# One turn of k^T v instead of two, and the gate's columns copied together with it

## The chip, the cores and the metric

The kernel runs on one core of one Trainium2 chip. The metric is the device time of one execution in microseconds (us). Times given as the kernel's time are medians over several executions; a profile shows one execution alone.

## What is computed

Linear attention without a softmax for 8 batches and 8 heads (576 positions, 64 columns a head), an RMS norm per head, and then a mixture of 8 experts on the 512 joined columns:

```python
kv = np.einsum('bhsd,bhse->bhde', k, v)
out = np.einsum('bhsd,bhde->bhse', q, kv)
rms = np.sqrt(np.mean(out * out, axis=-1, keepdims=True) + 1e-06)
x = out / rms * g_norm                   # heads joined to 512 columns
logits = np.einsum('bsd,de->bse', x, w_gate)
local_gate = 1.0 / (1.0 + np.exp(-np.einsum('bsd,de->bse', x, w_local).squeeze(-1)))
# per position: the best expert if local_gate < 0.5 or s == 0, else the expert of the position before
h = np.maximum(x[b, s] @ w1[e], 0.0)
out[b, s] = p[e] * (h @ w2[e])           # p: softmax of the logits
```

## The kernel before

There are two stages. The first computes attention, the gate and the routing, and writes rows to a table `xs` in DRAM. The second gathers rows by expert and multiplies them with the experts' matrices.

The first stage runs in 16 steps `s` (NST). A step takes two batches and two heads, that is 4 products of 64x64 each. `kv(s)` multiplies k^T v into PSUM (tile `po`) and copies it to `kvp`: on partitions 64y to 64y+63, in column block x, stands the product of head x and batch x xor y. Each of the two heads' products is needed on both halves of the partitions, since q, turned by `turn_q` and `turn_last` into `qT` and `ql`, has even and odd positions on different halves. `kvb_of(s, t)` therefore copies `kvp` to half t of `kvb`, in two copies of 64 partitions on POOL (GpSimd), one per y.

Beside the 64 columns of each product `kvb` has NG = 9 more: the product times the gate's columns (8 experts and the local gate). So the multiplication q (k^T v) in `q_kv` delivers the logits, before the norm's factor, with the output. They are made from k^T v turned by 90 degrees: `turn_kv` turns `kvp` (128x128) on PE and ACT copies the result to `kq`; before the change it turns it twice, for each half t of the output partitions anew, so that `kq` has the product twice, side by side. `logits_of` multiplies `kq` with `gw`, the gate's columns scaled by `g_norm`, once for each half, into `pm`; two copies on ACT put the 2 x 9 columns each beside the products in `kvb`, on all 128 partitions.

PE, ACT (ScalarE), DVE (VectorE) and POOL follow an order written out by hand: the string `STEP` has one letter for each piece of work of step i, `LATE` has other strings for the last three steps, and `work_of` says what a letter does:

- Q, a: the first part of q (k^T v) for step i, and its copy to `raw`; c, R: the second part, and its copies
- K, k: k^T v for step i+2 on PE, and its copy to `kvp`; K also issues the loads of k and v for step i+4
- V: turns `kvp` of step i+2 and copies it to `kq`
- L, l: the logits product of step i+1 on PE, and its copy on ACT
- 0, 1: `kvb_of` for step i+1, halves 0 and 1
- T, U: turn q of step i+1; e: load q for step i+3
- x, y, X, Y: squares of the output for the norm, on POOL or on ACT; s: their sums on DVE
- p, m, q, b: pieces of norm, gate and routing of a finished group of four steps; w, v: split a piece of an expert's matrix; o: store three rows' blocks and load a piece
- G, 2, 3, 4, 5: the first two gathers for the experts, and their scaling and turning

Loads and stores are issued on SP in the order of the program; at most 7 are under way at a time (`LANES`). PSUM has three buffers for the tiles `pq`, `pl`, `pt`, `pm` (`ps_q`) and two for `po`. `HW` is 64 + 9 = 73, `XO` is 9, `slot(x, b)` is the column in `kvb` at which head x of batch b begins, and `pair` views two equal pieces of a tile at a fixed distance.

Of the kernel before, what the change touches and what calls it, by code (L numbers as in the profile page):

```python
# [8 lines left out]
F32 = mybir.dt.float32  # L9
# [13 lines left out]
def kernel(  # L23
# [12 lines left out]
    nc = tc.nc  # L36
    P = 128
    B, H, S, D = q.shape
# [3 lines left out]
    NG = E + 1  # L42
# [5 lines left out]
    NP = H // 2  # L48
    HW = D + NG
    PW = 2 * HW  # L50
    KB = PW - NG
    XO = NG
    NGRP = B // 2
    NCH = NGRP * C
    NST = NGRP * NP
# [23 lines left out]
    ident = const.tile([P, P], F32, name="ident")  # L79
# [63 lines left out]
    KVB, LGC = "PP", "A"  # L143
# [5 lines left out]
    wk = work.enter_context(tc.tile_pool(name="wk", bufs=2, reuse_waits="tile"))  # L149
# [10 lines left out]
    for src, e0 in ((w_gate, 0), (w_local, E)):  # L160
# [8 lines left out]
    ps_q = ps1.enter_context(tc.tile_pool(name="ps_q", bufs=3, space=PSUM,  # L169
                                           reuse_waits="tile"))  # L170
# [134 lines left out]
    gw = rc.tile([P, NP, 2 * NG], F32, name="gw")  # L305
# [55 lines left out]
    kvps, kvbs, kqs, qTs, qls = {}, {}, {}, {}, {}  # L361

    def half(b):
        return slice(b * D, (b + 1) * D)

    def kv(s):


        pk = ps_o.tile([P, 2, 512], F32, name="po")
        ks, vs = ([t.pop((s, b)) for b in range(2)] for t in (kts, vts))  # L370
        for c in range(C):
            cd = slice(c * D, (c + 1) * D)
            for b in range(2):
                for x in range(2):
                    nc.tensor.matmul(pk[half(x ^ b), x, 0:D], ks[b][half(x), cd],  # L375
                                     vs[b][half(x), cd], start=(c == 0), stop=(c == C - 1))
        yield
        kvps[s] = wk.tile([P, 2, D], F32, name="kvp")
        nc.scalar.copy(kvps[s], pk[:, :, 0:D])  # L379
        yield  # L380

    def pair(t, o0, o1, n):

        w = o1 - o0
        return t[:, o0:o0 + 2 * w].rearrange("p (x w) -> p x w", w=w)[:, :, 0:n]


    def slot(x, b):
        return (2 * (x ^ b) + x) * HW

    def kvb_of(s, t):

        if s not in kvbs:
            kvbs[s] = wk.tile([P, 2 * HW + 2 * (HW + D)], F32, name="kvb", bufs=3)
        for y in range(2):
            copy[KVB[t]](pair(kvbs[s][half(t)], slot(0, y) + XO, slot(1, 1 - y), D),  # L396
                         kvps[s][half(y)])

    copy = {"A": nc.scalar.copy, "D": nc.vector.tensor_copy, "P": nc.gpsimd.tensor_copy}

    def turn_kv(s):

        pt = ps_q.tile([P, 2, P], F32, name="pt", tag="pq")
        kvp = kvps[s].rearrange("p x d -> p (x d)")
        for t in range(2):
            nc.tensor.transpose(pt[:, 0:2, half(t)], kvp, ident)
        kqs[s] = wk.tile([P, 2, P], F32, name="kq", bufs=3)
        nc.scalar.copy(kqs[s], pt)

    def turn_last(s):  # L410
# [6 lines left out]

    def logits_of(s):

        pm = ps_q.tile([P, 2, 2 * NG], F32, name="pm", tag="pq")  # L420
        for y in range(2):
            nc.tensor.matmul(pm[:, y], kqs[s][:, y], gw[:, s % NP], start=True, stop=True)
        yield
        for y in range(2):
            copy[LGC](pair(kvbs[s], slot(0, y), slot(1, 1 - y) + D, NG),
                      pm[:, y].rearrange("p (x e) -> p x e", x=2))
        yield

    def turn_q(s, b):
# [410 lines left out]
    LOADED = {i: j for j, i in enumerate((1, 2, 3, 4, 5, 9, 13, 14))}  # L840
    SPLIT = {i: j for j, i in enumerate((4, 5, 7, 8, 10, 12, 15))}

    STEP = "QKasw1p0kcRTUeqLlmvVxobY"
    LATE = {NST - 3: "QKswLpck01qaRmGXVvlYbTUeo", NST - 2: "QKLmapkRUcT10q2lVe3Ysxbo", NST - 1: "5Q4wRcvsaxyO"}

    SLOTS = {}
    for g in range(NGRP - 1):
# [11 lines left out]
    def work_of(i, what):  # L859
# [16 lines left out]
        elif what in "ac" and now:  # L876
            next(step[what])
            done.add((i, what))
        elif what == "K" and new:
            step["k"] = kv(i + 2)  # L880
            next(step["k"])
            for b in range(2):
                load_kv(i + 2 + LB, b)
        elif what == "k" and new:
            next(step["k"])
        elif what == "L" and nxt:
            step["l"] = logits_of(i + 1)
            next(step["l"])
        elif what == "l" and nxt:
            next(step["l"])  # L890
        elif what in "01" and nxt:
            kvb_of(i + 1, int(what))
        elif what == "T" and nxt:
            for b in range(2):
# [3 lines left out]
        elif what == "e" and nxt:  # L898
            assert i + 1 in qls and i + 1 in qTs
            for b in range(2):  # L900
                load_q(i + 1 + LQ, b)
        elif what == "V" and new:
            turn_kv(i + 2)
        elif what == "w" and i in SPLIT:
            step["v"] = wsplit(0, SPLIT[i], True)
# [30 lines left out]
    for i in range(-2, NST):  # L936
        if i == NST - 1:
            paced.clear()
        if i == NST - 2:
            xb = rw.tile([P, C, NP * PW], F32R, name="raw", bufs=3).rearrange("p c w -> p (c w)")  # L940
            xh, xl = (xb[:, o:o + ND * 2 * P].rearrange("p (d t) -> p d t", d=ND)
                      for o in (0, ND * 2 * P))
        for what in LATE.get(i, STEP):
            work_of(i, what)
# [518 lines left out]
```

## Time and profile before

| what | value |
|---|---|
| median of 3 runs | 583.35 us (582.9 to 585.02) |
| the profiled execution's own time | 580.4 us |
| its span on the core | 578.6 us |
| PE busy | 540.2 us (93%) |
| PE weight loads busy | 480.8 us (83%) |
| DVE, ACT, POOL busy | 306.9, 239.2, 235.3 us |
| DMA packets | 41380, 94.97 MB, mean 164 GB/s |

The span is the stretch of the profiled execution that the profiler shows; the execution's own time is 1.8 us longer. In rows of the profile, L12 is line 12 of the kernel; PE is the matrix engine's products, PEld its weight loads; `out<-in` names the tiles; `[x <-y]` is the idle time of the engine just before, and what ended it; "issue" is waiting for nothing that the profile shows. A product of 32-bit numbers stands as two weight loads and two matmuls, a transposition as one of each.

### The profile page before, as it was taken

How to read it: one execution, taken by the hardware profiler on the slowest of the kernel's cores; microseconds unless marked ns; L12 is line 12 of the kernel's file. 1: busy time of each engine (PE TensorE's matmuls, PEld its weight loads, DVE VectorE, ACT ScalarE, POOL GpSimd, SP SyncE). 2: the span in 40 equal slices, each digit the busy share in tenths (PEclk: the TensorE clock that was granted, in tenths of full speed). 3: DMA queues.
4: the chain of work that ended last, by engine and by line, in shares of the span. 5: the costliest groups of instructions: out<-in, count | busy, mean ns of one | idle time of the engine just before them, and what ended most of it. 6: DMA issues, size and time to landing. Idle time of an engine off the chain costs nothing. (4 is left out here: it accounts for less than half of the span.)

```text
span 578.6 us, 12798 instructions
## 1 busy us (share of the span) xinstructions
PE 540.2 (93%) x5157; PEld 480.8 (83%) x5157; DVE 306.9 (53%) x627; ACT 239.2 (41%) x435; POOL 235.3 (41%) x303
## 2 busy tenths in 40 slices
PE   2987978779999999999999999999999999999996
PEld 2876866759887989899898998989898979999895
DVE  1126578688866633725363755374546545564510
ACT  1567767472244433332343343333433333435220
POOL 4233454133236725434363573456344734442001
PEclk9988899799999999999999999999999999999999
DMA  7999999871657344233443343345343533432000
GB/s 227 342 316 355 295 375 376 291 248 52 237 194 284 102 159 143 89 104 105 130 124 112 110 154 97 123 137 162 86 132 115 172 98 123 145 105 80 18 20 30
DMA packets 41380, 94.97 MB, mean 164 GB/s; under 512 B 7263, under 2 KB 7263, under 8 KB 41312
## 3 DMA queue, kind: packets, MB, share of 16 engines
q1 hardware_dynamic: 32032, 72.64, 36.7%
q0 software_dynamic: 7744, 21.41, 12.4%
q8 instruction: 42, 0.69, 0.5%
q10 hardware_dynamic: 1536, 0.02, 0.1%
q14 instruction: 26, 0.21, 0.1%
HBM read 73.85 MB, written 20.86 MB: 164 GB/s over the span
## 5 line engine op out<-in xcount | busy, mean ns | idle before, releaser
L780 POOL DMA_INDIRECT xr<-xs,gid x120 | 132.1, 1101 | 36.6 <-issue 33.6
L1032 DVE SCALAR_TENSOR_TENSOR hl<-ph,hh 128x384 fp32r<-128x384 f32 (+3 forms) x92 | 52.2, 568 | 115.4 <-ACT hh L1031 111.9
L997 POOL DMA_INDIRECT out_dram<-ot,sidr x34 | 33.8, 994 | 176.9 <-ACT ot L996 136.3
L1031 ACT ACTIVATE hh<-ph 128x384 fp32r<-128x384 f32 (+3 forms) x92 | 47.0, 510 | 124.4 <-PE ph L967 124.4
L996 ACT ACTIVATE ot<-py,pe 128x512 f32<-128x512 f32 (+1 forms) x37 | 25.5, 689 | 70.5 <-PE py L967 31.9
L495 POOL TENSOR_TENSOR sq<-raw 128x576 f32<-128x576 f32 x16 | 19.3, 1210 | 59.4 <-ACT raw L465 30.8
L375 PE MATMUL po<-vt,kt 64*64 64x64 f32 x1152 | 26.6, 243 | 14.1 <-DMA vt<-in_v_dram 10.8
L500 DVE TENSOR_REDUCE ms<-sq 128x9 f32<-128x576 f32 x32 | 23.1, 748 | 28.1 <-POOL sq L495 22.1
L375 PEld LDWEIGHTS po<-vt,kt 64*64 64x64 f32 x1152 | 24.4, 157 | 14.8 <-issue 10.3
L456 PE MATMUL po<-kvb,qT 64*64 64x73 f32 x1024 | 29.2, 246 | 7.5 <-issue 6.7
L456 PEld LDWEIGHTS po<-kvb,qT 64*64 64x64 f32 x1024 | 23.6, 148 | 13.6 <-issue 9.0
L396 POOL COPY kvb<-kvp 64x128 f32<-64x128 f32 x64 | 22.4, 349 | 16.3 <-ACT kvp L379 10.2
L462 ACT COPY raw<-po 128x876 f32<-128x876 f32 (+1 forms) x32 | 20.7, 648 | 19.7 <-PE po L456 19.1
L808 DVE TENSOR_TENSOR xr<-xr 128x512 f32<-128x512 f32 x37 | 25.4, 686 | 0.2 <-DMA xr<-xs,gidr 0.2
L801 ACT CAST yh<-xT 128x512 fp32r<-128x512 f32 x17 | 10.5, 620 | 29.5 <-DVE xT L797 29.5
L961 PE MATMUL py<-w_0h,hh 128*128 128x512 f32 (+1 forms) x56 | 22.2, 397 | 0.0
L966 PE MATMUL py<-w_0l,hh 128*128 128x512 f32 (+1 forms) x56 | 22.1, 394 | 0.0
L961 PE MATMUL py<-w_1h,hh 128*128 128x512 f32 (+1 forms) x56 | 22.1, 394 | 0.0
L967 PE MATMUL py<-w_0h,hl 128*128 128x512 f32 (+1 forms) x56 | 22.0, 393 | 0.1
L435 PE MATMUL pq<-ident,qt 128*128 128x128 f32 x128 | 19.5, 295 | 2.6 <-DMA wst<-in_moe_w_dram 2.1
L966 PE MATMUL py<-w_1l,hh 128*128 128x512 f32 (+1 forms) x56 | 21.9, 391 | 0.0
L967 PE MATMUL py<-w_1h,hl 128*128 128x512 f32 (+1 forms) x56 | 21.8, 390 | 0.0
(433 smaller groups left out, 1661.0 us busy)
## 6 DMA issues: line engine op xcount, KB each, us to landing
wst<-in_moe_w_dram SPq DMA_DIRECT2D x64, 512.0 KB, 3.7
xs<-raw SPq DMA_DIRECT2D x36, 292.0 KB, 5.4
kt<-in_k_dram SPq DMA_DIRECT2D x32, 288.0 KB, 5.2
vt<-in_v_dram SPq DMA_DIRECT2D x32, 288.0 KB, 5.2
qt<-in_q_dram SPq DMA_DIRECT2D x32, 288.0 KB, 5.1
xr<-xs,gid POOLq DMA_INDIRECT x120, 4.5
out_dram<-ot,sidr POOLq DMA_INDIRECT x36, 4.0
xr<-xs,gidr POOLq DMA_INDIRECT x6, 5.5
```

Of the source, the lines that this page charges most:

```text
L375: nc.tensor.matmul(pk[half(x ^ b), x, 0:D], ks[b][half(x), cd], vs[b][half(x), cd], start=(c == 0), stop=(c == C - 1))
L456: nc.tensor.matmul(po[half(b), r, o:o + HW], lhsT[half(r), half(x)], kvb[half(r), slot(x, b):slot(x, b) + HW], start=True, stop=True)
L500: nc.vector.tensor_reduce(mss[g][:, :, 2 * n + x], sqs.pop((s, x)), axis=AX.X, op=ALU.add)
L780: i = nc.gpsimd.indirect_dma_start(out=xr[:, u * PW:(u + 1) * PW], out_offset=None, in_=xs.rearrange("t (q w) -> (t q) w", w=PW), in_offse ...
L808: (engine or nc.vector).tensor_mul(xv, xv, r.unsqueeze(3).to_broadcast([P, NP, 2, D]))
L961: mm = nc.tensor.matmul(ps, ah, bh, start=(first and i == 0), stop=False)
L966: nc.tensor.matmul(ps, ah, bl, start=False, stop=False)
L967: nc.tensor.matmul(ps, al, bh, start=False, stop=(last and i == n - 1))
L996: nc.scalar.activation(ot[0:m], po[0:m], AF.Copy, scale=pe[0:m])
L997: return nc.gpsimd.indirect_dma_start(out=outf, out_offset=bass.IndirectOffsetOnAxis(ap=idx[0:m], axis=0), in_=ot[0:m], in_offset=None, bo ...
L1031: nc.scalar.activation(hh, ps, AF.Relu)
L1032: nc.vector.scalar_tensor_tensor(hl, ps[:, :, 0:nl], 0.0, hh[:, :, 0:nl].bitcast(F32), op0=ALU.max, op1=ALU.subtract)
```

## The change

`turn_kv` turns k^T v once, and `kq` has 128 columns instead of 256. `logits_of` multiplies it once, into 2 x 9 columns, and one copy on ACT puts these beside the products in `kvp`, which has room for them now: 9 columns ahead of the first product and 9 behind the second. `kvb_of` then copies products and logits together, 146 neighbouring columns instead of twice 64, and so follows the logits' copy now. In `STEP` the logits product (L) moves from behind the turning of q to behind k^T v (K), its copy (l) moves from the end of the step to behind the copy of k^T v (k), and the copies to the halves (1, 0) come behind that. `LATE` is changed likewise.

```diff
-        kvps[s] = wk.tile([P, 2, D], F32, name="kvp")
-        nc.scalar.copy(kvps[s], pk[:, :, 0:D])
+        kvps[s] = wk.tile([P, 2 * (HW + D)], F32, name="kvp")
+        nc.scalar.copy(kvps[s][:, XO:XO + 2 * D].rearrange("p (x d) -> p x d", x=2), pk[:, :, 0:D])
...
     def kvb_of(s, t):
+        assert s in lgs
         if s not in kvbs:
-            kvbs[s] = wk.tile([P, 2 * HW + 2 * (HW + D)], F32, name="kvb", bufs=3)
+            kvbs[s] = wk.tile([P, 4 * HW], F32, name="kvb", bufs=3)
         for y in range(2):
-            copy[KVB[t]](pair(kvbs[s][half(t)], slot(0, y) + XO, slot(1, 1 - y), D),
-                         kvps[s][half(y)])
+            copy[KVB[t]](kvbs[s][half(t), slot(0, y):slot(0, y) + 2 * HW],
+                         kvps[s][half(y), 0:2 * HW])
...
     def turn_kv(s):
-        pt = ps_q.tile([P, 2, P], F32, name="pt", tag="pq")
-        kvp = kvps[s].rearrange("p x d -> p (x d)")
-        for t in range(2):
-            nc.tensor.transpose(pt[:, 0:2, half(t)], kvp, ident)
-        kqs[s] = wk.tile([P, 2, P], F32, name="kq", bufs=3)
+        pt = ps_q.tile([P, P], F32, name="pt", tag="pq")
+        nc.tensor.transpose(pt, kvps[s][:, XO:XO + 2 * D], ident)
+        kqs[s] = wk.tile([P, P], F32, name="kq", bufs=3)
         nc.scalar.copy(kqs[s], pt)
...
     def logits_of(s):
-        pm = ps_q.tile([P, 2, 2 * NG], F32, name="pm", tag="pq")
-        for y in range(2):
-            nc.tensor.matmul(pm[:, y], kqs[s][:, y], gw[:, s % NP], start=True, stop=True)
+        pm = ps_q.tile([P, 2, NG], F32, name="pm", tag="pq")
+        nc.tensor.matmul(pm.rearrange("p x e -> p (x e)"), kqs[s], gw[:, s % NP],
+                         start=True, stop=True)
         yield
-        for y in range(2):
-            copy[LGC](pair(kvbs[s], slot(0, y), slot(1, 1 - y) + D, NG),
-                      pm[:, y].rearrange("p (x e) -> p x e", x=2))
+        copy[LGC](pair(kvps[s], 0, HW + D, NG), pm)
+        lgs.add(s)
         yield
...
-    STEP = "QKasw1p0kcRTUeqLlmvVxobY"
-    LATE = {NST - 3: "QKswLpck01qaRmGXVvlYbTUeo", NST - 2: "QKLmapkRUcT10q2lVe3Ysxbo", NST - 1: "5Q4wRcvsaxyO"}
+    STEP = "QKLaswpkl01cRTUeqmvVxobY"
+    LATE = {NST - 3: "QKLswpckl01qaRmGXVvYbTUeo", NST - 2: "QKLmapkl01RUcTq2Ve3Ysxbo", NST - 1: "5Q4wRcvsaxyO"}
```

More of the change, by code (lines that the diff above doesn't have):

```diff
@@ L391, in kvb_of @@
     def kvb_of(s, t):
+        assert s in lgs
         if s not in kvbs:
-            kvbs[s] = wk.tile([P, 2 * HW + 2 * (HW + D)], F32, name="kvb", bufs=3)
+            kvbs[s] = wk.tile([P, 4 * HW], F32, name="kvb", bufs=3)
         for y in range(2):
-            copy[KVB[t]](pair(kvbs[s][half(t)], slot(0, y) + XO, slot(1, 1 - y), D),
-                         kvps[s][half(y)])
+            copy[KVB[t]](kvbs[s][half(t), slot(0, y):slot(0, y) + 2 * HW],
+                         kvps[s][half(y), 0:2 * HW])
+    lgs = set()
     copy = {"A": nc.scalar.copy, "D": nc.vector.tensor_copy, "P": nc.gpsimd.tensor_copy}
     def turn_kv(s):
-        pt = ps_q.tile([P, 2, P], F32, name="pt", tag="pq")
-        kvp = kvps[s].rearrange("p x d -> p (x d)")
-        for t in range(2):
-            nc.tensor.transpose(pt[:, 0:2, half(t)], kvp, ident)
-        kqs[s] = wk.tile([P, 2, P], F32, name="kq", bufs=3)
+        pt = ps_q.tile([P, P], F32, name="pt", tag="pq")
+        nc.tensor.transpose(pt, kvps[s][:, XO:XO + 2 * D], ident)
+        kqs[s] = wk.tile([P, P], F32, name="kq", bufs=3)
         nc.scalar.copy(kqs[s], pt)
```

## The prediction

> **What bounds the kernel now.** I read the page's first line, then the busy time by stretches, to see in which stretch a saved microsecond counts.
>
> ```profile
> span 578.6 us, 12798 instructions
> ```
> ```profile
> 17.00:107.00 90.00, 72.67 (x2119) 63.65 (x2114) 48.52 (x103) 61.60 (x153) 33.21 (x64) 0.94 0.98 345
> 107.00:129.00 22.00, 18.34 (x362) 15.56 (x361) 16.81 (x44) 14.69 (x39) 7.58 (x14) 0.85 0.72 232
> 129.00:578.60 449.60, 443.46 (x2540) 396.66 (x2540) 239.48 (x473) 161.00 (x241) 188.43 (x173) 1.00 0.38 121
> ```
>
> The columns are length, busy PE, weight loads, DVE, ACT, POOL (count in brackets), granted clock, DMA share, GB/s. From 129 us on, the experts' products keep PE busy 443.46 of 449.60 us at full clock: the change touches nothing there, so whatever the attention stage ahead of it wins or loses reaches the end whole. In that stage PE is busy 72.67 of 90 us while DMA is at 0.98. Which of them sets the pace? PE's own list of waits over the first 130 us says what PE lacked (columns: total us, times, longest).
>
> ```profile
> PE po L375 <- DMA vt<-in_v_dram: 10.8, 4, 5.6
> PE po L456 <- issue: 9.8, 5, 3.1
> ```
> ```profile
> PEld po L456 <- ACT kvb L425: 3.6, 14, 0.3
> PEld pm L422 <- ACT qT L436: 3.0, 11, 0.4
> ```
>
> ```profile
> 15.08 2.19 PE L375 MATMUL po<-vt,kt 64*64 64x64 f32 x68 [1.67 <-DMA vt<-in_v_dram]
> ```
>
> The waits for v are four, and this is the last: after some 15 us the loads are ahead of PE. The two small ones with ACT are the ones the change touches: 3.6 us for logits copied into `kvb`, 3.0 us for a free PSUM buffer of the logits. The large one is "issue", in which PE waits for nothing that the profile names. I cut the stretch where those gaps end, and asked for the DMA queues of the first 130 us.
>
> ```profile
> q8 instruction: 20, 0.33, 1.0%
> ```
> ```profile
> 58.77:73.60 14.83, 14.00 (x382) 12.39 (x381) 8.67 (x23) 11.96 (x31) 6.41 (x13) 0.88 0.91 304
> ...
> 84.44:89.26 4.83, 4.60 (x127) 4.02 (x127) 2.17 (x5) 3.84 (x10) 2.30 (x5) 1.00 1.05 382
> 89.26:94.90 5.64, 4.64 (x127) 4.06 (x127) 4.91 (x16) 5.30 (x14) 2.38 (x5) 1.00 1.04 364
> 94.90:101.10 6.20, 4.61 (x128) 3.90 (x128) 5.55 (x12) 3.40 (x10) 2.40 (x5) 1.00 1.05 392
> 101.10:106.94 5.84, 2.79 (x127) 2.57 (x127) 3.25 (x9) 2.00 (x3) 0.00 (x0) 0.98 1.05 386
> sum 80.94, PE 64.16 PEld 56.41 DVE 47.57 ACT 55.06 POOL 29.75; mean PE 5.83 PEld 5.13 DVE 4.32 ACT 5.01 POOL 2.70
> ```
>
> Between two such gaps PE always runs 127 or 128 weight loads and as many matmuls (three times that in the first row): 256 instructions. Queue q8 brought 20 packets of together 0.33 MB, so 16 KB each, one for every 256. PE stops at these boundaries until the next piece of its program has come through DMA engines that are full. From 26 to 107 us there are 15 pieces in 80.94 us, 5.40 us each, while PE is busy only 64.16 us. So over most of that stretch the pace is the arrival of PE's instructions, some 5 to 6 us a piece, and what PE saves inside a piece becomes a longer stop, unless pieces hold more work. The three pieces from 58.77 on, 4.94 us each, were hardly delayed: there PE's own work is the pace.
>
> [...]
>
> **The change part by part.** For each of 16 pair-steps:
>
> ```profile
> 23.51 0.38 PE L414 MATMUL pl<-ident,qt 128*128 128x128 f32 x2
> 23.91 0.62 PE L422 MATMUL pm<-gw,kq 128*128 128x18 f32 x4
> 24.40 0.44 PE L406 MATMUL pt<-ident,kvp 128*128 128x128 f32 x2
> 24.85 0.68 PE L456 MATMUL po<-kvb,qT 64*64 64x73 f32 x25
> ```
>
> (1) PE loses one transposition of two (L406) and two of the four records of L422 (one logits product of two). That is 3 pairs of weight load and matmul a step. From 23.91 to 24.85 logits, transposition and the two waits take 0.94 us. Without them the next Q.KV could follow the transpositions of q by about 0.35 us (two of L414's rank and one of L406's; L422's remaining half moves ahead to a place where PE would else run on, about 0.25). So PE alone could gain up to 0.94 - 0.35 = 0.6 us a step.
>
> (2) Is something else late then? The same place in a later step, ACT and POOL beside it:
>
> ```profile
> 63.90 0.27 ACT L379 COPY kvp<-po 128x128 f32<-128x128 f32 x1 [0.21 <-PE po L375]
> ...
> 65.10 1.07 ACT L436 COPY qT<-pq 128x512 f32<-128x512 f32 x2
> ...
> 66.45 1.58 POOL L396 COPY kvb<-kvp 64x128 f32<-64x128 f32 x4
> 66.49 0.26 ACT L425 COPY kvb<-pm 128x18 f32<-128x18 f32 x2
> ...
> 66.82 0.99 PE L456 MATMUL po<-kvb,qT 64*64 64x73 f32 x48
> ```
>
> The second qT copy ends at 66.17, and Q.KV needs it: it can start at about 66.2 instead of 66.82, and if the logits copy, now ahead of qT's copies on ACT, pushes them by its 0.18, at 66.35. So 0.5 to 0.6 us a step is all that there is; the next thing late is ACT's qT. I take 0.5.
>
> (3) The added wait: POOL's copies to the halves (0, 1) now wait for ACT's logits copy, which stands behind kvp's copy. ACT is done with both at 63.90 + 0.27 + 0.18 = 64.35. POOL's four copies, at some 0.33 us with their gaps, are through by 65.75 (the wider 146 columns at worst 146/128 of that, 65.9): before qT at 66.17, so at nothing. Behind them on POOL stand the square product of the step (up to 1 us later than now, for sums that DVE reads a step afterwards), and in the late steps the gathers (next part). Behind the logits copy on ACT stand the copies of Q.KV's second part and of qT: the 0.18 above. POOL's added columns come to at most 64 x 0.05 = 3 us in all, beside other work. ACT's shorter turned copy (256 to 128 columns) and one small copy less are a gain that I count in (2). The logits product early on PE needs the turned copy of the step before, long done after Q.KV and K.V. No DMA is added, removed or passed on SP; `kvb` shrinks and `kvp` grows, with no load in it.
>
> (4) How much survives the stops? Start of the chain: the first delayed boundary follows one or two steps of PE-paced work: +0.5 us (0 to 1.0). The pieces not delayed, four or so: each holds 0.8 of a step, so up to 0.4 us apiece, 1.6 in all; I take 0.4, as shortening them meets the arrival time soon. Then the pieces hold more work. By the last delayed boundary, in step 12, the changed kernel has dropped 14 transpositions and 26 products' pairs: 40 pairs. At the mean pace that is 40/128 x 5.40 = 1.7 us. But what these 40 pairs are at that boundary can be read off:
>
> ```profile
> 106.95 0.75 PE L456 MATMUL po<-kvb,ql 64*64 64x73 f32 x8 [3.05 <-issue]
> 107.63 1.97 PE L435 MATMUL pq<-ident,qt 128*128 128x128 f32 x8
> 109.39 0.63 PE L414 MATMUL pl<-ident,qt 128*128 128x128 f32 x2
> ...
> 111.13 0.65 PE L456 MATMUL po<-kvb,qT 64*64 64x73 f32 x12
> ```
>
> After the stop of 3.05 us they take from 106.95 to 111.13, 4.2 us, at half speed (L414's two take 0.63 against 0.38 above). With the boundary moved 40 pairs on, this work, its ACT copies included, falls into what is now the 3.05 us stop and the next Q.KV begins near the boundary. So this term lies between 1.7 and 4.2; I take 3.6, near the row that shows the very work, less 0.6 for instructions that come later because q loads and stores move into the full DMA stretch (pieces above vary by 4.83 to 6.20).
>
> (5) The tail. The transposition L414 at 109.39 releases the last q loads on SP, behind which stand row stores and a weight load, and the gathers on POOL wait for the stores:
>
> ```profile
> 117.66 1.23 POOL L770 DMA_INDIRECT xa<-xs,gi  x1 [6.76 <-DMA wst<-in_moe_w_dram]
> ...
> 123.66 0.74 POOL L396 COPY kvb<-kvp 64x128 f32<-64x128 f32 x1 [3.11 <-DMA xa<-xs,gi]
> ```
>
> So what step 12 wins moves the gather, and with it the last copies to `kvb`, which wait for the landed gather before and after the change. The logits copy no longer follows them: about 0.25 us.
>
> **Sum:** 0.5 + 0.4 + 3.6 + 0.25 = 4.75 us, bounds 0 + 0 + 1.7 + 0 and 1.0 + 1.6 + 4.2 + 0.4. The profiled execution took 580.4, its span and 1.8 around it, so 575.65; the median of the runs is 2.95 above it, and to it the forecast is 583.35 - 4.75 = 578.6.
>
> **The rivals.** *Swallowed:* the stops take back all but the smaller count: 1.7 + 0.5 = 2.2 us, 581.2. For it speaks that most of the 15 pieces were delayed; against it the 4.2 us of real work after the last stop. A variant with no gain at all (the boundaries fall badly, 583) gets a little.
>
> *All passes:* the instructions arrive sooner with PE's boundaries, and every step gives 0.6: 9.6 us, 573.8. Against it: DMA is at 1.04 in the rows from 84 us on, and the same bytes must pass.
>
> *Slower, by POOL:* the copies now lie between the logits and Q.KV, and POOL can be held up.
>
> ```profile
> 78.78 3.36 POOL L396 COPY kvb<-kvp 64x128 f32<-64x128 f32 x4
> ...
> 80.19 1.45 DVE L740 TENSOR_TENSOR lo<-lane,iota_l 128x1152 bf16<-128x1152 int32 x1
> ```
>
> Here four copies took 3.36 us beside DVE products of two SBUF inputs. It is hidden now because POOL runs a step ahead; afterwards 64.35 + 3.36 = 67.7 would hold Q.KV 1.35 us past 66.35. The gain is gone when that strikes 4.75/1.35 = 3.5 steps of 16, and at 6 the kernel is slower by over 0.5%; at 8 of 16 it ends at 583.35 - 4.75 + 10.8 = 589.4. Seen so far in two or three steps. [...]
>
> **How the numbers follow.** Forecast (576.0 to 580.4) 0.45, swallowed 0.25, no gain 0.07, all passes 0.13, POOL 0.10. A change of 0.5%, 2.9 us, is about what a measurement here can tell from none. Faster: forecast, all passes and a little of the swallowed case, 0.60; same 0.29; slower 0.11. The range 574 to 584 leaves out POOL's case and part of "all passes".
>
> **What would show it.** Right: L406 x16 and L422 x32; 20 or 19 packets on q8, still 127 or 128 pairs between stops; no wait of L456 for logits; the step after the last stop starting with Q.KV, near 106; the first gather near 113 instead of 117.66; equal busy time behind it. Wrong: stops that are longer by what PE saved and a gather still at 115 or later (swallowed); waits of L456 for POOL's copies above 1 us (slower); pieces under 4.8 us (all passes).

## The result: slower by 0.9%, nearly all of it ahead of the experts

The changed kernel takes 588.41 us (median of 20 runs), the kernel before 583.0 us beside it on the same chip (20 runs): a ratio of 1.0093, 95% interval 1.0071 to 1.0114, some 5.4 us slower where 4.75 us of gain were forecast. The ratios leave out executions more than 1.5% above the fastest of the same kernel, of after here one of 593.5 us. The profiled execution took 589.14 us, 8.7 more than that of before: it lies 0.7 us above its median, and that of before 2.6 below, so 3.3 us of the difference between the two profiles belong to this pair of executions. Its span, and the busy time by stretches (length, busy PE, weight loads, DVE, ACT, POOL, granted clock, DMA share, GB/s):

```profile
span 587.3 us, 12689 instructions
```
```profile
17.00:107.00 90.00, 71.04 (x1839) 62.45 (x1842) 38.30 (x81) 52.02 (x128) 30.35 (x59) 0.87 0.89 303
107.00:137.30 30.30, 24.30 (x600) 20.76 (x590) 26.62 (x66) 20.09 (x49) 12.64 (x23) 0.89 0.84 285
137.30:587.30 450.00, 443.49 (x2540) 396.76 (x2540) 239.35 (x472) 160.80 (x241) 189.90 (x173) 1.00 0.38 122
```

The last row is the last row of before again (443.46 of 449.60 us): of the 8.7 us, 8.3 lie in the attention stage. In the same 90 us the queues now bring 303 GB/s instead of 345, at a share of 0.89 instead of 0.98, and PE does 1839 matmuls instead of 2119. The experts' first product comes at 135.72 us instead of 127.60. The stretch from 17 us to that product, in before and then in after:

```profile
17.00:127.60 110.60, 90.63 (x2478) 79.02 (x2473) 63.95 (x143) 74.89 (x189) 40.78 (x78) 0.92 0.93 321
```
```profile
17.00:135.72 118.72, 94.96 (x2424) 83.03 (x2423) 63.36 (x143) 70.53 (x173) 42.98 (x82) 0.87 0.88 297
```

Length less busy time gives PE's idle time: 19.97 us before, 23.76 after. Of the 8.1 us, 3.8 are more idling. The other 4.3 are more busy time for 54 matmuls fewer, at a granted clock of 0.87 instead of 0.92. The bytes are alike (110.60 us at 321 GB/s are 35.5 MB, 118.72 at 297 are 35.3).

The work that was to go has gone, as the groups of lines show (busy us, mean ns, then the idle time ahead of them):

```profile
L397 POOL COPY kvb<-kvp 64x146 f32<-64x146 f32 x64 | 23.4, 366 | 72.6 <-ACT kvp L425 65.7 <-DVE rk L692 2.7 <-DMA xa<-xs,gi 1.4
L422 PE MATMUL pm<-gw,kq 128*128 128x18 f32 x32 | 7.0, 297 | 0.0
L407 PE MATMUL pt<-ident,kvp 128*128 128x128 f32 x16 | 5.8, 361 | 0.6 <-ACT kvp L379 0.4
```
```profile
q8 instruction: 19, 0.31, 1.0%
```

POOL now waits 65.7 us for the logits' copy (L425) ahead of its own copies; that is the added wait. In PE's list of waits over the first 130 us it hardly appears:

```profile
PEld po L375 <- issue: 18.6, 6, 5.5
...
PEld po L456 <- issue: 15.3, 14, 3.4
...
PE po L456 <- issue: 12.4, 8, 3.2
...
PE po L375 <- issue: 8.4, 3, 5.0
...
PEld po L456 <- POOL kvb L397: 0.6, 3, 0.3
```

What rose is "issue": ahead of the matmuls of Q.KV (L456) from 9.8 to 12.4 us, and ahead of the weight loads of K.V (L375) from 10.3 to 18.6 us (behind 17 us, from 3.3 to 8.8). A wait for a load of q, k or v stands in neither list of PE's behind 17 us. Who keeps the loads back shows in SyncE's own queue from 17 to 125 us, in before and then in after (total, times, longest):

```profile
SPq L186 <- PE po L375: 16.9, 10, 2.9
SPq L186 <- PE pl L414: 9.4, 5, 4.7
```
```profile
SPq L186 <- PE pm L422: 12.7, 5, 4.3
SPq L186 <- PE pl L415: 11.2, 6, 4.5
...
SPq L186 <- PE po L375: 5.7, 4, 2.8
...
SPq L186 <- PE pt L407: 4.4, 4, 2.9
```

A load needs a buffer that PE has finished with, so where PE stops the queue can stand too: these rows come to 26.3 us in before and 34.0 in after. That this is how the stream got slower is a reading of these lists, tested in experiment 8.

### The profile page after: what moved, and what is told of

Its sections match the earlier page's. It is cut to its first block, busy times and chain, and to the rows that moved or that the text cites. A ratio compares the mean times of both kernels' runs of the same rounds, so it can differ in the third digit from the quotient of the medians.

```text
span 587.3 us, 12689 instructions
## 1 busy us (share of the span) xinstructions
PE 544.9 (93%) x5109; PEld 485.2 (83%) x5109; DVE 306.4 (52%) x627; ACT 235.0 (40%) x419; POOL 237.8 (40%) x303
## 4 chain that ended last, share of the span: by engine, by line
PE 84%; issue 6%; DMA 5%; DVE 3%; POOL 1%; ACT 1%; POOLq 0%; SPq 0%; ACTq 0%
PE ph L966 12%; PE ph L961 12%; PE ph L967 12%; PE py L961 11%; PE py L966 11%; PE py L967 11%; PE po L456 5%; PE po L375 3%; PE pq L435 3%; PE py L1011 1%; DMA xr<-xs,gidr 1%; DMA qt<-in_q_dram 1%; PE pm L422 1%; DMA out_dram<-ot,sidr 1%; DMA vt<-in_v_dram 1%
## 5 line engine op out<-in xcount | busy, mean ns | idle before, releaser
L397 POOL COPY kvb<-kvp 64x146 f32<-64x146 f32 x64 | 23.4, 366 | 72.6 <-ACT kvp L425 65.7
L375 PE MATMUL po<-vt,kt 64*64 64x64 f32 x1152 | 26.9, 244 | 18.9 <-DMA vt<-in_v_dram 10.5
L456 PE MATMUL po<-kvb,qT 64*64 64x73 f32 x1024 | 34.3, 254 | 9.9 <-issue 9.5
L375 PEld LDWEIGHTS po<-vt,kt 64*64 64x64 f32 x1152 | 24.8, 158 | 19.9 <-issue 18.6
L456 PEld LDWEIGHTS po<-kvb,qT 64*64 64x64 f32 x1024 | 26.5, 152 | 16.2 <-issue 12.6
L462 ACT COPY raw<-po 128x876 f32<-128x876 f32 (+1 forms) x32 | 20.8, 649 | 26.7 <-PE po L456 26.3
L435 PE MATMUL pq<-ident,qt 128*128 128x128 f32 x128 | 22.3, 331 | 0.0
```

The costliest lines, as they stand in the source:

```text
L435: nc.tensor.transpose(pq[:, w], qts[s, b][:, w * P:(w + 1) * P], ident)
L456: nc.tensor.matmul(po[half(b), r, o:o + HW], lhsT[half(r), half(x)], kvb[half(r), slot(x, b):slot(x, b) + HW], start=True, stop=True)
```

## The experiments

All ratios are to the kernel before on the same chip. "Without loads" means that q, k and v are loaded for the first two steps only. In these kernels only the stage up to the experts' first product is read; lines are 7 higher (L463 is Q.KV, L382 K.V, L429 the logits, L404 POOL's copies).

**1. The three pairs back.** The kernel after, with turn and logits product made twice into the same tiles, so 160 pairs a step again.

```diff
-        nc.tensor.transpose(pt, kvps[s][:, XO:XO + 2 * D], ident)
+        for _ in range(2):
+            nc.tensor.transpose(pt, kvps[s][:, XO:XO + 2 * D], ident)
...
-        nc.tensor.matmul(pm.rearrange("p x e -> p (x e)"), kqs[s], gw[:, s % NP],
-                         start=True, stop=True)
+        for _ in range(2):
+            nc.tensor.matmul(pm.rearrange("p x e -> p (x e)"), kqs[s], gw[:, s % NP],
+                             start=True, stop=True)
```

> The changed kernel with PE's work put back: k^T v is turned twice into the same tile and the logits product is done twice into the same tile (the second writes the same values again), so that PE has 160 pairs of weight load and matmul a step as before the change; the new order, the new data flow and the copies stay. Theory A (stops: the change moved the 256-instruction boundaries of PE's program, from 160 pairs a step to 157, against the bursts of loads, and instructions now come later): boundaries fall as before the change, so the time goes back to 583 (581.5 to 585), and the experts' products start near 129 us of the span. Theory B (order: the moved logits, or the wait of POOL's copies for them, delays each step): nothing of that is undone, so 588 or more, up to 593 as PE also has 0.3 us a step more to do.

Ratio 1.0161 (1.0117 to 1.0205). Putting the count back brings nothing back.

**2. The logits late again,** with after's data flow: the copies to the halves then stand right ahead of the Q.KV that needs them.

```diff
-    STEP = "QKLaswpkl01cRTUeqmvVxobY"
+    STEP = "QKaswpkcRTUeqLl01mvVxobY"
```

> The changed kernel's data flow (157 pairs a step) with the logits product and its copy back in their old places behind the turning of q, and the two half copies behind them (the last three steps keep the changed order). Theory A (stops): the count of instructions, not the order, is what hurts: 586 to 591. Theory B (order): the cause is undone, 583 or below, unless Q.KV waits for POOL's 1.4 us of copies at the end of each step, which would show as waits of L456 for POOL of about 1 us in 12 steps.

Its six runs took 592.68 us or more, against 588.66 for before, and no interval can be given; the profiled span is 597.5 us. By these this order is no better, but it pays for POOL's copies in full, so it says nothing on after's own order. From 17 to 130 us:

```profile
PE po L456 <- POOL kvb L397: 10.7, 19, 1.2
```

**3. Both kernels without loads.** Only the first tiles are loaded:

```diff
-        if s < NST:
+        if LB <= s < NST:
+            kts[s, b], vts[s, b] = first[s % LB, b]
+        elif s < NST:
```

> The kernel before the change without the loads of q, k and v from step 2 on: the tiles of steps 0 and 1 are used again (the output is that of repeated inputs, and the routing and the second stage differ; only the first stage's trace is read). Theory A: with DMA mostly idle PE's instructions come in time, so the stops go from about 1.6 us a piece to under 0.5, and the first stage ends 15 to 25 us earlier. Theory B: no statement on the stops; the stage is as long as PE's and ACT's work.

> The changed kernel without the loads of q, k and v from step 2 on, as in the run beside it (output and routing of repeated inputs; the first stage's trace alone is read). Theory A (stops): with the stops gone the smaller work on PE counts, and the changed kernel's steps are shorter than the other's by 0.3 to 0.6 us, 5 to 9 us over the stage. Theory B (order): its steps are longer than the other's by 0.3 to 0.5 us, whatever DMA does.

First product at 109.85 us (before) and 117.37 us (after), 17.75 and 18.35 us sooner than with loads; the distance stays, 7.5 us.

```profile
17.00:109.85 92.85, 85.70 (x2488) 74.84 (x2482) 63.30 (x143) 73.55 (x189) 44.62 (x78) 0.96 0.34 114
```
```profile
17.00:117.37 100.37, 87.85 (x2431) 75.80 (x2426) 62.27 (x143) 70.45 (x173) 43.89 (x82) 0.93 0.31 104
```

Idle time is 7.15 us against 12.52, so most of the difference (5.4 of 7.5 us) is PE standing still, with the queues at 0.34 and 0.31: loads standing ahead of PE's instructions are not the whole cause. This trace also shows POOL's copies late for Q.KV in some steps (POOL, then PE, in after without loads):

```profile
48.18 2.28 POOL L404 COPY kvb<-kvp 64x146 f32<-64x146 f32 x4 [4.02 <-ACT kvp L432]
```
```profile
49.47 1.96 PE L463 MATMUL po<-kvb,qT 64*64 64x73 f32 x47
```

The copies end at 50.46, so Q.KV's first part, begun at 49.47, takes 1.96 us instead of the 1.00 of before. That made a theory: late copies.

**4. Copies in time.** Twice: the logits, their copy and POOL's four copies right behind Q.KV's first part; or the four copies on DVE. And the first one without loads.

```diff
-    STEP = "QKLaswpkl01cRTUeqmvVxobY"
+    STEP = "QKLla01swpkcRTUeqmvVxobY"
```
```diff
-    KVB, LGC = "PP", "A"
+    KVB, LGC = "DD", "A"
```

> The kernel after with one edit of the order: the logits' product, their copy on ScalarE and the four GpSimd copies of a step stand at once behind Q.KV's first part ("QLKla01swpkc...") instead of behind K.V and its copy ("QKLaswpkl01c..."). Instructions, widths and waits are as many as before. Theory "late copies": after the change the four copies may start only when ScalarE has copied the logits, which stands behind K.V, so they end about when the next Q.KV begins; its first four weight loads then wait for one copy each, and what is lost there (up to 1 us a step, in most of the steps) is the 8 us. Here the copies start some 2.5 us sooner, so no weight load of Q.KV waits for GpSimd, and the first expert product moves from 137.3 us to 129 or before: the time falls to 0.985 to 1.002 of the kernel before. Rival "fetches": the loss is where the 256-instruction pieces of TensorE's program end in the step, with the half clock behind each stop; the order of TensorE's products is nearly the same here (one weight load and product moved by 36), so the first expert product stays at 134 to 139 us and the ratio at 1.005 to 1.013.

> The kernel after with the four copies that widen k^T v on VectorE instead of GpSimd, the order unchanged. The theory "late copies" has two parts: the copies start late (behind the logits copy), and they are slow and shared (366 ns each on GpSimd, 1.5 to 2.3 us for four). VectorE's copies should take about 0.2 us each (its 128x72 operations take 0.23), so they end about 0.8 us behind the logits copy instead of 1.5 to 2.3, before the next Q.KV unless VectorE is in its routing work (long operations of 0.5 to 1.8 us, some steps of each group). So: half or more of the 8 us comes back, first expert product at 129 to 133 us, ratio 0.995 to 1.004. If the loss is the place alone (any wait behind the logits copy), or VectorE's routing work holds the copies, it stays at 1.005 or more; by the rival "fetches" it stays at 1.005 to 1.013 too, without a wait of Q.KV for the copies.

> The kernel early without the loads of q, k and v from the third step on (the first tiles are used again, so the values differ); read in the first stage alone. In the two kernels without loads the first expert product was at 109.85 us (before) and 117.36 us (after). "Late copies": 107 to 111 us here, steps of 4.8 to 5.6 us, Q.KV's 48 pairs in 0.83 us as without a wait. "Fetches": 115 us or later.

Early: 1.0088 (1.0057 to 1.0119), first product at 132.23 us. On DVE: 1.0066 (1.0034 to 1.0099), at 129.88. Early without loads: 113.61, in between. The waits for POOL were taken away (0.2 us are left in each list of PE's weight loads) and the ratio hardly fell, so late copies are at most a smaller part. The one profile of the kernel with DVE would have said otherwise: its first product came in the range that "late copies" expected, its ratio did not. (In early the program's order puts the logits ahead of K.V on PE.) The traces without loads say why the work saved is not even won where PE is undisturbed. One such step of before, and one of early:

```profile
30.32 1.00 PE L463 MATMUL po<-kvb,qT 64*64 64x73 f32 x45
31.13 0.21 PE L382 MATMUL po<-vt,kt 64*64 64x64 f32 x1
...
34.38 0.62 PE L429 MATMUL pm<-gw,kq 128*128 128x18 f32 x4
34.87 0.44 PE L413 MATMUL pt<-ident,kvp 128*128 128x128 f32 x2
35.32 0.35 PE L463 MATMUL po<-kvb,qT 64*64 64x73 f32 x2
```
```profile
24.49 1.31 PE L463 MATMUL po<-kvb,qT 64*64 64x73 f32 x48
25.73 0.40 PE L429 MATMUL pm<-gw,kq 128*128 128x18 f32 x2
26.05 1.28 PE L382 MATMUL po<-vt,kt 64*64 64x64 f32 x72
...
29.18 0.33 PE L414 MATMUL pt<-ident,kvp 128*128 128x128 f32 x1
29.44 0.27 PE L463 MATMUL po<-kvb,qT 64*64 64x73 f32 x1
```

From Q.KV to Q.KV it is 5.00 us in before and 4.95 in early, though logits and turn became cheaper (0.94 us from 34.38 to 35.32; 0.26 from 29.18 to 29.44 and 0.32 for L429). K.V began 0.81 us behind Q.KV, running in between its last products; now L429 comes 1.24 behind it and K.V 1.56. In the trace's single instructions a semaphore instruction of its own stands between Q.KV's first weight loads: the second load starts at 24.54, the third only at 24.78. It waits for ACT's second copy of qT, which ends at 24.66; POOL's copies for this step had ended at 22.83. In before the same copy ends at 34.81, and Q.KV begins 0.5 us behind it:

```profile
33.74 1.07 ACT L443 COPY qT<-pq 128x512 f32<-128x512 f32 x2
```

And L429's weight load, 128 rows wide, starts 0.21 us behind the last 64-row one (25.51, 25.73).

**5. The order alone, and the order mended.** Border is the kernel before, only with the logits moved. Ahead_tick is the kernel after with logits a step further ahead among the 128-row products, and a small ACT copy (t) that reads the finished `kvb`, meant to let Q.KV wait for one engine alone.

```diff
-    STEP = "QKasw1p0kcRTUeqLlmvVxobY"
+    STEP = "QKLasw1p0klcRTUeqmvVxobY"
```
```diff
-    STEP = "QKLaswpkl01cRTUeqmvVxobY"
+    STEP = "Q01KaswpkcRVtTUeqLlmvxobY"
...
-        elif what == "L" and nxt:
-            step["l"] = logits_of(i + 1)
+        elif what == "L" and new:
+            step["l"] = logits_of(i + 2)
...
+        elif what == "t" and nxt:
+            tk = wk.tile([P, 1], F32, name="tk")
+            nc.scalar.copy(tk, kvbs[i + 1][:, 4 * HW - 1:4 * HW])
```

> The kernel before, with all of its instructions, its 160 pairs and its early GpSimd copies; one edit of the order: the logits' weight loads and products (L) stand between Q.KV's first part and K.V instead of behind the turns of q, and their ScalarE copy (l) behind K.V's copy ("QKLasw1p0klcRTUeqmvVxobY" for "QKasw1p0kcRTUeqLlmvVxobY"). Theory "place of the logits on TensorE": without loads, in the kernel early, the undisturbed step was 4.95 us against 5.01 in before although 0.45 us of TensorE's work was gone, because L's 128-row weight load stood 0.21 us behind the last 64-row load of Q.KV (25.505 to 25.717) and K.V began only after it, where in before K.V's loads run in between Q.KV's last ones. So the step grows by 0.2 to 0.4 us: ratio 1.003 to 1.012, first expert product 2 to 6 us later than in before (129.06). Rival "GpSimd's copies" (late copies and Q.KV's waits for them are the whole loss): none of it is here, so 0.998 to 1.002.

> The kernel after with the logits one step further ahead: K.V's turn, its logits and their copy for step i+2 are all made in step i, among the 128-row products ("VTUL"), and the four GpSimd copies for i+1 stand at the start of step i ("Q01KaswpkcRVtTUeqLlmvxobY"); and a ScalarE copy of one column of the widened k^T v (t, 128x1) stands ahead of the copies of the turned q, so that Q.KV's weight loads have one engine to wait for, as in before. Still three pairs fewer a step than before. "Place of the logits": both costs are gone (the 0.21 us and the lost overlap between Q.KV and K.V; 0.24 us for a semaphore instruction of its own between Q.KV's first weight loads), the three pairs' 0.45 us come through: undisturbed steps of 4.5 to 4.7 us, and the time is 0.985 to 0.999 of before. Rival "fetches": TensorE's program comes in pieces of 256 instructions, 2.35 us each and the delay ahead of it; denser steps only move the waits to these, so the time stays at 1.000 to 1.010, with stops of 25 us or more in the first stage. Rival "GpSimd's copies" expects the same as the first.

> The kernel border without the loads of q, k and v from the third step on (the first tiles are used again, so the values differ); read in the first stage alone. "Place of the logits": undisturbed steps of 5.2 to 5.4 us (before without loads: 5.01), first expert product at 112 to 116 us (109.85). "GpSimd's copies": 5.0 us and 109 to 111 us.

> The kernel ahead_tick without the loads of q, k and v from the third step on (the first tiles are used again, so the values differ); read in the first stage alone. "Place of the logits": undisturbed steps of 4.5 to 4.7 us, Q.KV's first 24 pairs 0.76 us from their first weight load to the next product's instead of 1.24, first expert product at 103 to 109 us (before 109.85, after 117.36, early 115.0). "Fetches": undisturbed steps are that short too, but what they win is waited for again at the pieces of 256 instructions: 109 us or later, and the gaps above 0.3 us at the pieces add up to more than before's 5 us by what was won.

Border: 1.0103 (1.0057 to 1.015). The move costs what the whole change costs, with before's work and early copies; but its pieces lie elsewhere too, since a step has 324 instructions on PE instead of 322. (The logits stand behind K.V in the trace, not ahead of it as the expectation says.) Without loads its first product is at 116.99 us, but its undisturbed step, 43.45 to 48.54, is 5.09 us, 0.09 more than before: 1.4 us over 16 steps, of 7.1. So the expected 0.2 to 0.4 us a step did not show, and the theory "place of the logits" gives the sign and not the size.

Ahead_tick: 1.0032 (0.9996 to 1.0068), better than after and no gain over before. Without loads:

```profile
25.52 1.18 PE L463 MATMUL po<-kvb,qT 64*64 64x73 f32 x45
...
30.25 0.27 PE L463 MATMUL po<-kvb,qT 64*64 64x73 f32 x1
```
```profile
17.00:115.18 98.18, 82.73 (x2448) 73.18 (x2441) 63.84 (x145) 70.21 (x188) 45.89 (x78) 0.95 0.33 111
```

Here the saving is real: steps of 4.73 us, and 2.97 us less busy time than before (85.70). But PE stands idle for 15.45 us instead of 7.15, and the first product comes at 115.18. What the shorter step wins is waited for again and more, about half of it (3.9 us) where pieces end, where "fetches" expected it, the rest for other engines. In this trace too Q.KV's third weight load (25.75) follows the end of ACT's second qT copy (25.63), so that wait is still there.

**6. The same kernel, its pieces moved.** Sixteen or 24 turns of the identity into an unused bank ahead of the first K.V, while PE waits for its first load. Nothing in any step changes, but each piece of 256 instructions ends 32 or 48 instructions sooner.

```diff
+    for _ in range(16):
+        nc.tensor.transpose(rbank[:, 128:128 + P], ident, ident)
     for i in range(-2, NST):
```

> The kernel before with 16 turns of the identity into an unused bank put ahead of the first K.V on TensorE, where it waits for the first load anyhow: 32 more instructions once, order and work of every step untouched, but each piece of 256 instructions now ends 32 instructions earlier in the step. (A step has 320 instructions, so four steps are five pieces and the places repeat: 0, 64, 128, 192, 256 and an offset.) "Fetches": where the pieces end in the step decides how long it stops, in either direction, and this change alone moves the first expert product by 2 us or more: ratio 0.990 to 0.996 or 1.004 to 1.012. "Order": what counts is which product stands behind which, 0.998 to 1.002.

> As before_pad16, with 24 turns of the identity ahead of the first K.V: the pieces of the kernel before are moved by 48 instructions. "Places of the pieces": each offset has its own time; if the kernel before stands at a favourable one, this is slower than it too, 1.002 to 1.010; if pad16 was an unfavourable one among many that are alike, 0.998 to 1.002. "Order alone": 1.000 within 0.002 (already spoken against by before_pad16, 1.0064).

1.0064 (1.0037 to 1.0091) and 1.0065 (1.0029 to 1.01). Two other places, and each costs 0.6% of the very kernel that was the base. With 16:

```profile
17.00:107.00 90.00, 73.09 (x2114) 64.08 (x2106) 47.07 (x99) 61.14 (x153) 34.94 (x64) 0.94 0.96 335
```
```profile
26.93 1.22 PE L375 MATMUL po<-vt,kt 64*64 64x64 f32 x70
28.10 0.48 PE L456 MATMUL po<-kvb,qT 64*64 64x73 f32 x16
28.42 0.22 PE L456 MATMUL po<-kvb,ql 64*64 64x73 f32 x1
32.85 0.47 PE L456 MATMUL po<-kvb,ql 64*64 64x73 f32 x7 [4.21 <-issue]
```

In this step one piece held nearly all of Q.KV and K.V, the stretch densest in instructions: it was through in 2.4 us (26.24 to 28.64), and PE stood 4.21 us for the next. The stream falls from 345 to 335 GB/s. The stops as such are hardly longer in total: up to the first product PE is idle for 17.9 us at the ends of pieces with 16 turns and 17.3 with 24, against 16.8 in before (from the single instructions). In these two profiles that product comes at 132.48 and 131.87 us, and the larger parts of the loss are elsewhere: with 16, PE waits 3.78 us for the gathered rows instead of 1.47; with 24, it is busy 94.05 us at a granted clock of 0.88 instead of 90.63 at 0.92.

**7. Fewer loads in flight,** 4 for 7, in three kernels.

```diff
-    LB, LQ, LANES = 2, 2, 7
+    LB, LQ, LANES = 2, 2, 4
```

> The kernel before with at most 4 instead of 7 loads of q, k and v in flight (LANES, 0.29 MB each: 1.18 MB instead of 2.06 MB). In before the fetch of a piece of TensorE's program started 2.9 us (mean of 14) behind the crossing into the piece ahead of it, 1.2 us where 0.3 MB were outstanding and 3.7 where 1.5 MB were. Theory "fetches behind loads": with less outstanding a fetch starts sooner (mean 2.2 us or less), the stops at the pieces fall from 20 us to 14 or less and the half clock behind them with it, so the stage gets shorter: ratio 0.985 to 0.998, first expert product at 121 to 128 us (129.06). Rival "loads bind": the queues were busy 0.98 of the stage at 345 GB/s; four in flight leave them idle between, the stage gets longer: 1.000 to 1.02.

> The kernel after with at most 4 instead of 7 loads of q, k and v in flight. In after a fetch started 3.5 us (mean of 12) behind the crossing. "Fetches behind loads": the loss came from stops, so it shrinks with them: 0.985 to 1.003 of before, and 0.98 to 0.995 of after. "Loads bind": 1.005 to 1.02 of before.

> The kernel ahead_tick (three pairs fewer a step, logits among the 128-row products, copies a step ahead, one wait in Q.KV; 1.0032 of before) with at most 4 instead of 7 loads in flight. "Fetches behind loads": its undisturbed step of 4.73 us (without loads) against 5.01 in before comes through as the stops shrink: 0.975 to 0.997 of before, the fastest of the four. "Loads bind": 1.000 to 1.02.

1.0359 (1.033 to 1.0387), 1.0373 (1.0336 to 1.041) and 1.0385 (1.0353 to 1.0416). The mechanism that was expected is there: in before_l4 a fetch starts 1.84 us behind the crossing (mean; 2.90 on the mean of 14 in before), and PE's idle time at the ends of pieces falls from 16.8 to 5.6 us. Yet the kernel is 21 us slower:

```profile
17.00:107.00 90.00, 70.92 (x1856) 62.08 (x1854) 40.37 (x87) 56.65 (x140) 30.16 (x59) 0.91 0.87 283
```
```profile
SPq L186 <- DMA vt<-in_v_dram: 17.5, 26, 2.6
SPq L186 <- DMA qt<-in_q_dram: 16.0, 24, 1.7
SPq L186 <- DMA kt<-in_k_dram: 15.5, 24, 2.2
```

SyncE's queue now waits for its own loads, the stream is down to 283 GB/s, and the three kernels are equal within their intervals. "Loads bind" was right for this run. But PE's list shows a wait that neither before nor after has behind 17 us (17 to 130 us of before_l4):

```profile
PE po L375 <- DMA vt<-in_v_dram: 17.1, 15, 2.6
```

So fewer loads in flight put one limit in the place of another, and the run does not say which of the two bound the kernel before.

**8. One more pair of q tiles,** in after and in ahead_tick, to let the loads run through a stop.

```diff
-    LB, LQ, LANES = 2, 2, 7
+    LB, LQ, LANES = 2, 3, 9
...
-            kvbs[s] = wk.tile([P, 4 * HW], F32, name="kvb", bufs=3)
+            kvbs[s] = wk.tile([P, 4 * HW], F32, name="kvb", bufs=2)
```

> The kernel after with a third pair of q tiles (LQ 3 for 2, up to 9 loads in flight for 7, and two buffers of the widened k^T v for three to make room): q for a step is loaded one step sooner, so SyncE's queue, which waited for TensorE's turns of q and the logits' product (12.7 + 11.2 us in the first stage), stops less when TensorE stops. Theory "holes in the loads": after lost because TensorE's stops at its pieces keep buffers and so the next loads back; with one more pair ahead the stream is fuller (320 to 345 GB/s from 17 to 107 us for 303) and half or more of the 5 us comes back: ratio to before 0.990 to 1.004. Rival "TensorE itself": its own stops and half clock set the time and the loads follow: 1.006 to 1.012, the stream still at about 305 GB/s. More outstanding loads could also make each fetch start later: then above 1.010.

> The kernel ahead_tick (1.0032 of before) with the same third pair of q tiles. "Holes in the loads": 0.985 to 1.000 of before, the stream at 330 GB/s or more (310 in ahead_tick). "TensorE itself": 1.000 to 1.006.

1.0074 (1.0027 to 1.0121) and 1.01 (1.0057 to 1.0144). The stream in the 90 us rose to 330 GB/s in both, as expected, and the time did not follow. PE's idle time at the ends of pieces is 19.1 us in after_q3 and 22.6 in ahead_q3. (`kvb` has a buffer fewer here, so this edit moves more than the loads.) This one speaks against holes in those 90 us as the whole account. No version beat the kernel before.

## Why the prediction was wrong

**What bounds the stage.** The prediction read "so over most of that stretch the pace is the arrival of PE's instructions". The runs bear this out in part: without loads PE's idle time at the ends of pieces falls from 16.8 to 3.8 us, and the first product comes 17.75 us sooner. They do not separate it from the other candidate, the queues at 0.98: the run without loads changed both (the queues at 0.34, and a fetch 1.18 us behind its crossing on the mean instead of 2.79), and the run with fewer loads in flight made loads the limit itself. That the pieces come "through DMA engines that are full" was the author's estimate from the 0.98: the fetches stand on q8 and the loads on q1, and no view shows one waiting for the other. So this reading is not the step that is shown to have failed. What failed is what the prediction made of it in term (4), and the size of terms (1) and (2).

**Terms (1) and (2), 0.5 us a step.** In after, without loads, the undisturbed step is 4.87 us (24.90 to 29.77) for 5.00. In these rows of that trace L429 is the logits product, L443 the qT copy:

```profile
27.18 0.40 PE L429 MATMUL pm<-gw,kq 128*128 128x18 f32 x2
27.51 0.48 PE L463 MATMUL po<-kvb,qT 64*64 64x73 f32 x16
...
28.87 1.07 ACT L443 COPY qT<-pq 128x512 f32<-128x512 f32 x2
...
29.77 0.34 PE L463 MATMUL po<-kvb,qT 64*64 64x73 f32 x2
```

That "the next thing late is ACT's qT" was right, and so was what could be won up to it: Q.KV's third weight load stands 0.58 us behind the end of the second qT copy in before and 0.11 behind it in after, which is 0.47 us. But from Q.KV's second part to that end it is 2.43 us in both kernels (32.38 to 34.81 in before, 27.51 to 29.94 here), and the half of the logits product that stays now stands ahead of that second part, 0.33 us (27.18 to 27.51). It pushes the turn of q, its copies and the next Q.KV by as much in every step. "L422's remaining half moves ahead to a place where PE would else run on, about 0.25" counted it on PE and left it out of the chain that leads to qT. So 0.13 us is left of 0.5. The other undisturbed steps follow the same sum: in early the logits stand in that chain too (4.95), in border both halves do (5.09), and in ahead_tick neither does, but the turn of k^T v (4.73).

**Term (3), the added wait at nothing.** In size nearly right, in mechanism not: the copies are late in some steps (1.96 us for 1.00), but kernels without that wait are at 1.0088 and 1.0066. The rival "slower, by POOL" forecast the sign by a mechanism that is not the main carrier.

**Term (4), 3.6 us at the last stop.** This carried the forecast, and it is the step that failed in sign: in the two profiles the stops did not shrink, they grew by 5.5 us, and the time at half clock with them. The table, from the single instructions and clock records, is for 17 us to the experts' first product (us); "at pieces" is PE's idle time that ends with the first instruction of a piece.

| | before | after | before, 16 turns | before, 24 turns |
|---|---|---|---|---|
| PE idle, at pieces | 16.8 | 22.3 | 17.9 | 17.3 |
| PE idle, elsewhere | 3.2 | 1.4 | 5.8 | 3.5 |
| PE busy | 90.6 | 95.0 | 91.8 | 94.1 |
| time at a granted clock of 0.5 | 17.1 | 30.7 | 20.3 | 26.6 |

So PE's other idle time did shrink (3.2 to 1.4 us), but longer stops and more time at half clock took more than that. The prediction moved the pieces by 40 pairs and looked only at the one place where that helps. Moving them by 16 or 24 pairs with no other edit costs 0.64% and 0.65%. Two thirds of the 0.93% is the size of such a shift, and the intervals overlap. The case "the boundaries fall badly, 583" got 0.07, and no loss was allowed for it; it should have been one of the main rivals, with both signs. The fetches show how little stood between PE and a badly placed boundary: each began only behind the crossing into the piece ahead of its own (1.15 to 4.14 us behind it in before, 1.06 to 5.80 in after), so in these two profiles one piece at most lay ready.

**Term (5), the tail.** From the first gather to the first product it is 9.94 us in before (117.66 to 127.60) and 9.33 in after:

```profile
126.39 1.23 POOL L770 DMA_INDIRECT xa<-xs,gi  x1 [4.85 <-DMA wst<-in_moe_w_dram]
```

The 0.25 us is there and more (0.6), but at 126.39 and not near 113.

**What stays open.** That after loses because its pieces fall elsewhere is argued, not shown: its step has 157 pairs and a semaphore instruction more (317 instructions for 322), so its pieces drift through the step, and no kernel was run that gives after the places of before. The kernel of experiment 1 has 323 and is no faster, so the count alone is not the cause. The loss without loads (7.1 us in border, 5.9 of them idle time, 13.03 us against 7.15) shows that the stops differ by the order even with the queues at a third: at pieces 9.9 us against 3.8, and 8.1 in after. What sets the moment at which a fetch begins was not found.

## What to carry to other kernels

Before costing an edit, follow the chain that the moved piece joins: PE had less to do here, but the logits product now stood ahead of the turn of q, and so of ACT's copies for which the next Q.KV waits. Where two resources are both full, relieve one of them in an experiment, and look what the engine waits for then: with fewer loads in flight PE stopped less for its program (5.6 us for 16.8) and waited for loads instead (17.1 us). In a long unrolled program, shift the instructions once without changing them (a few idle products at the start) and take the spread as the error bar of every edit: here it was 0.6%, two thirds of what the change cost. And where profiles are compared, set each one's time beside the median of its kernel first: here 3.3 of 8.7 us lay in that.

## What the runs showed of the hardware

The stops at pieces of before and after lie 256 of PE's single instructions apart, or twice or three times that, and q8 brought 42 packets of together 0.69 MB in each of the two executions. From the start of a fetch packet on q8 to PE going on it is mostly 2.2 to 2.8 us at stops over 0.6 us, with loads or without (2.25 to 2.53 in before, 2.27 to 2.81 in after, 2.34 to 2.66 in border without loads). What varies is the delay ahead of it, behind the crossing into a piece: up to the first product it is 2.79 us on the mean of 18 fetches in before and 1.18 without loads, 3.39 and 2.14 in after. But it also varies with the queues at 0.32, from 0.57 to 3.42 us in border without loads. The clock records of before and after know two values, 1.0 and 0.5, and up to the first product the half clock comes in stretches of 3.41 us (three in each) or 6.83 (one in before, three in after). Such a stretch stands behind some stops and not behind others: in after one from 64.38 to 67.79 us, behind the stop that ends at 63.90; in before none behind the stop that ends at 84.44, 3.14 us long. From 17 us to the first product the clock was 0.92 on the mean in before and 0.88 in before_pad24. Between Q.KV and K.V, both of 64-row tiles, weight loads mixed in before without loads (K.V's first, at 31.07, stands ahead of three of Q.KV's); in early without loads the 128-row load behind Q.KV began 0.21 us after the last 64-row one.
